# Where three weight tiles of a first layer are converted: beside that layer's own tiles, or between the joins of the second layer's first half

## The chip, the cores and the metric

One core of a Trainium2 chip runs the whole program. The metric is device time in microseconds (us). Engines are named as the profile names them: PE is the tensor engine (PEld its weight loads), DVE the vector engine, ACT the scalar engine, POOL the GpSimd engine, SP the engine from whose queue nearly all DMA transfers are issued.

## The reference

Four batch elements of 768 tokens go through two blocks.

```python
# block 1: 8 heads of 64 channels; each query sees its neighbours closer than 16 tokens,
# and 24 summaries (maximum of keys, mean of values over blocks of 32 tokens)
a = softmax([scale * q @ k.T within the window, scale * q @ k_sum.T + log(32)])
x = a @ [v, v_sum]                        # laid out as (4, 768, 512)
# block 2
u = x + real(fft(fft(x, axis=1), axis=2))
un = (u - mean(u)) / sqrt(var(u) + 1e-6)
out = u + maximum(un @ w_ch1, 0) @ w_ch2  # w_ch1 512 x 2048, w_ch2 2048 x 512
```

The two weight matrices arrive as 64-bit floats. The kernel turns them into 32-bit floats itself, once, while it works on the first batch element.

## The kernel before, in words

**The work of a batch element.** Attention by pairs of heads (`scores`, `sum_scores`, `values`), the two Fourier transforms and the normalisation (`gen_fourier`), the first layer (`gen_hidden`) and the second layer (`gen_out`). Each layer is done in two halves: `gen_hidden(b, 0)`, `gen_out(b, 0)`, `gen_hidden(b, 1)`, `gen_out(b, 1)`. Attention of the next batch element runs between them; in the stretch that matters here that is batch element 1, its last pair of heads (`p_1_3`), beside the layers of batch element 0.

**The layers.** Both layers use Strassen's scheme with seven products in place of eight (in the form with shared sums), so each weight tile is stored as seven blocks: four of the matrix, of which one is overwritten, and sums of them. The first layer's hidden units are cut into eight tiles j = 0 to 7, each with one weight tile `w1_0_j`. `gen_hidden(0, 0)` does tiles 0 to 3, `gen_hidden(0, 1)` tiles 4 to 7: seven products each, into PSUM banks `hx`, `hy`, `hz` (L1450), with copies and Relu on ACT (L1461, L1466, L1468, L1458, L1477) and additions on DVE (L582, the helper `tt`). The second layer has eight weight tiles `w2_0_j` likewise; `gen_out(0, 0)` contracts over tiles 0 to 3 and `gen_out(0, 1)` over 4 to 7.

**The second layer's first half, `gen_out(0, 0)`.** It has three row steps. The first is plain, since the sums of `w2` are not there yet: two PSUM banks (`o_0_0_0`, `o_0_0_3`, L1721), each added into `x` by one DVE instruction. Then row steps i = 1 and 2 do seven products each (L1746) into banks `ox`, `oy`, `oz`, and after each product a *join* on DVE adds the bank into `x`. The bank X is used by four products of a row step in turn, so each of them can begin only when the join of the one before has read it. There are four such banks in all (`bank`, `bufs=4`), and the bank of `o_0_0_3` is the one that the first product of row step 2 gets. Between the plain step and the rows DVE also makes the last sum T3 of each `w2` tile, and SP then stores the sums (`dw2_j`, 768 KB each).

**A conversion.** `convert(m)` turns one tile of 64-bit words into 32-bit floats. Its instructions on 128 x 1024 elements are: mask of the exponent bits (DVE, L1174), their shift (ACT, L1175), mask of the mantissa (DVE, L1187), its scaling (ACT, L1188), sign onto exponent (DVE, L1190), low word added (DVE, L1192), and the product (DVE, L582). `make` then adds three sums on DVE (L582, `_left_sums`). The raw words lie in a ring of two (`words`): the two loads of tile m + 2 can be issued once L1192 of tile m has read its words. SP issues transfers in a fixed order, and a transfer that waits holds all behind it.

**What sets the order.** `plan` (L1151) lists the sixteen conversions in order, each with a stage. `gen_weights` does not hand out a conversion before its stage is in `issued`. If the stage also has an entry in `marks`, the conversion's instructions are queued behind that instruction on the same engine (`tc.issue_after`). A scheduler then sets the order on each engine by what is handed out and by priority; each engine works strictly through its own list. Before the change, tiles 4, 5 and 6 of the first layer have the stages `("h", 0, 1)`, `("h", 0, 2)`, `("h", 0, 3)`, which are set at the end of tiles 1, 2, 3 of `gen_hidden(0, 0)`, and have no entry in `marks`.

## Time and profile before

| | |
|---|---|
| time, median of 3 runs | 794.03 us (792.45 to 794.19) |
| time of the profiled execution | 794.12 us |
| its span | 792.3 us (1.8 us lie outside the span) |
| PE, DVE, ACT busy | 767.6, 541.1, 248.9 us |
| mean clock granted to PE | 0.986 |

A row of the timeline gives the start, the duration, engine, line, operation, output and inputs, how many instructions were merged, and in brackets how long the engine sat idle before and whose end released it. A row of the windows gives, for a stretch of time, its length, the busy time of PE, PEld, DVE, ACT and POOL with the count of instructions, the clock granted to PE (1.00 is full), the share of the DMA engines and GB/s. One matrix product of the program is two records in the trace. The length of a record includes a tail that overlaps the next one; the time that a product takes of PE is the distance between starts.

### The profile page before, as it was taken

To read this page: it belongs to the slowest core of one execution; us is meant where nothing else is said; L and a number is where in the kernel's file an instruction comes from. 1 tells how busy PE (TensorE), PEld (TensorE's weight loads), DVE (VectorE), ACT (ScalarE), POOL (GpSimd) and SP (SyncE) were. 2 spreads that over 40 slices of the span, in tenths; PEclk is the share of its full clock that TensorE was granted. 3 is DMA by queue.
4 is the path that set the end of the run, shared out by engine and by line. 5 is a ranking of instruction groups with operands and counts; after the bars stand their busy time and mean duration, and the time that the engine had idled before them with its cause. 6 is when DMAs were issued, how large, how long until landed. Compare 5 with 4: busy or idle time off the path is not lost.

```text
span 792.3 us, 14996 instructions
## 1 busy us (share of the span) xinstructions
PE 767.6 (97%) x6068; PEld 591.0 (75%) x6068; DVE 541.1 (68%) x1145; ACT 248.9 (31%) x579; POOL 74.3 (9%) x102
## 2 busy tenths in 40 slices
PE   8999999869999999999999999999999999999997
PEld 5777555557569876688669876688659889889986
DVE  4789999976988825464576726463476987756762
ACT  3755657232535212200126112210116214203300
POOL 1000000000000002300030002300030004201500
PEclk8999999969999999999999999999999999999999
DMA  9897879695884359966244149820614034204001
GB/s 201 227 247 176 182 239 259 204 271 195 223 220 143 92 172 244 182 97 161 93 183 153 41 147 200 220 95 27 251 48 156 27 145 188 93 1 186 0 29 57
DMA packets 135901, 120.36 MB, mean 152 GB/s; under 512 B 94512, under 2 KB 117904, under 8 KB 135824
## 3 DMA queue, kind: packets, MB, share of 16 engines
q1 hardware_dynamic: 134672, 117.05, 53.6%
q0 software_dynamic: 576, 2.10, 0.8%
q8 instruction: 50, 0.82, 0.4%
q10 hardware_dynamic: 576, 0.17, 0.1%
q14 instruction: 27, 0.22, 0.1%
HBM read 97.28 MB, written 22.02 MB: 151 GB/s over the span
## 4 chain that ended last, share of the span: by engine, by line
PE 80%; DVE 12%; ACT 3%; DMA 2%; issue 1%; SPq 0%; DVEq 0%
PE ox L1746 19%; PE hx L1450 13%; PE oz L1746 10%; PE hz L1450 6%; PE oy L1746 5%; PE t L1619 4%; PE hy L1450 3%; PE y L1323 3%; DVE w L582 2%; PE f L1619 2%; PE mx L1282 2%; DMA words<-in_moe_w_ch_dram 2%; PE sc L810 2%; DVE w L1192 2%; PE sc L750 1%
## 5 line engine op out<-in xcount | busy, mean ns | idle before, releaser
L1450 PE MATMUL hx<-u,w 128*128 128x384 f32 x384 | 139.8, 492 | 1.2 <-ACT h L1461 0.8
L1450 PEld LDWEIGHTS hx<-u,w 128*128 128x128 f32 x384 | 71.1, 190 | 52.9 <-ACT p L817 3.7
L1746 PE MATMUL ox<-w,h 128*128 128x256 f32 x368 | 87.5, 382 | 4.1 <-DVE x L582 4.1
L1746 PE MATMUL ox<-w,s 128*128 128x256 f32 x368 | 89.3, 385 | 0.0
L1746 PE MATMUL oz<-w,s 128*128 128x256 f32 x368 | 89.0, 380 | 0.0
L1746 PEld LDWEIGHTS ox<-w,h 128*128 128x128 f32 x368 | 69.5, 191 | 16.1 <-DVE x L582 4.3
L1746 PEld LDWEIGHTS ox<-w,s 128*128 128x128 f32 x368 | 70.2, 193 | 10.6 <-DVE x L582 0.8
L582 DVE TENSOR_TENSOR x<-ox,x 128x256 f32<-128x256 f32 x92 | 38.9, 423 | 56.3 <-PE ox L1746 56.0
L1746 PEld LDWEIGHTS oz<-w,s 128*128 128x128 f32 x368 | 69.6, 190 | 9.5 <-DVE x L582 0.4
L1450 PE MATMUL hz<-u,w 128*128 128x384 f32 x192 | 70.3, 488 | 0.1
L1450 PEld LDWEIGHTS hz<-u,w 128*128 128x128 f32 x192 | 36.4, 190 | 25.6 <-DVE u L582 0.7
L1461 ACT COPY h<-hx 128x384 f32<-128x384 f32 x24 | 11.4, 476 | 114.0 <-PE hx L1450 114.0
L1746 PE MATMUL oy<-w,h 128*128 128x256 f32 x184 | 44.3, 381 | 0.7 <-ACT h L1668 0.7
L1622 ACT COPY f<-t 128x192 f32<-128x192 f32 x52 | 15.8, 303 | 78.3 <-PE t L1619 78.1
L582 DVE TENSOR_TENSOR x<-oz,x 128x256 f32<-128x256 f32 x46 | 19.5, 423 | 29.4 <-PE oz L1746 29.1
L1746 PEld LDWEIGHTS oy<-w,h 128*128 128x128 f32 x184 | 34.7, 190 | 6.2 <-ACT h L1668 1.5
L1598 POOL TENSOR_SCALAR h<-h 128x768 f32<-128x768 f32 x12 | 25.4, 2127 | 137.5 <-DVE h L1578 137.5
L585 POOL TENSOR_TENSOR vb<-vb 96x512 f32<-96x512 f32 (+2 forms) x20 | 20.4, 1022 | 174.2 <-DMA vb<-in_v_dram 173.2
L1450 PE MATMUL hy<-u,w 128*128 128x384 f32 x96 | 35.2, 488 | 1.5 <-DVE h L582 1.5
L582 DVE TENSOR_TENSOR s<-h 128x512 f32<-128x512 f32 x46 | 31.4, 682 | 0.9 <-ACT h L1458 0.6
L1477 ACT ACTIVATE h<-hx 128x384 f32<-128x384 f32 x24 | 11.7, 489 | 61.9 <-PE hx L1450 61.9
L582 DVE TENSOR_TENSOR h<-hy,h 128x384 f32<-128x384 f32 x24 | 13.3, 556 | 25.7 <-PE hy L1450 25.6
(236 smaller groups left out, 1310.5 us busy)
## 6 DMA issues: line engine op xcount, KB each, us to landing
w<-dw SPq DMA_DIRECT2D x46, 896.0 KB, 6.0
words<-in_moe_w_ch_dram SPq DMA_DIRECT2D x32, 512.0 KB, 6.0
dw<-w SPq DMA_DIRECT2D x12, 896.0 KB, 7.8
vw<-in_v_dram SPq DMA_DIRECT2D x47, 192.0 KB, 5.8
out_dram<-x SPq DMA_DIRECT2D x23, 256.0 KB, 2.0
vb<-in_v_dram SPq DMA_DIRECT2D x24, 192.0 KB, 8.1
kn<-in_k_dram SPq DMA_DIRECT2D x9, 384.0 KB, 6.4
qn<-in_q_dram SPq DMA_DIRECT2D x9, 384.0 KB, 7.2
```

Source lines behind the costliest of these rows:

```text
L582: return nc.vector.tensor_tensor(out=out, in0=in0, in1=in1, op=op).ins
L585: return nc.gpsimd.tensor_tensor(out=out, in0=in0, in1=in1, op=op).ins
L810: ins = nc.tensor.matmul(ps[h][r:r + 64, i, :], kt[rows, o:o + 64], qt[rows, o:o + BLOCK], start=True, stop=True)
L1192: nc.vector.scalar_tensor_tensor(out=dst, in0=low, scalar=2.0 ** -52, in1=dst, op0=ALU.mult, op1=ALU.add)
L1282: nc.tensor.matmul(out, y[:, g], table, start=False, stop=True, skip_group_check=True)
L1323: nc.tensor.matmul(y, fgs[b][par][:, st, P * g:P * (g + 1)], fs[par][:, g % 2, st, :], start=(st == 0), stop=(st == n - 1))
L1450: ins = nc.tensor.matmul(ps, w[:, a, kk, :], u[:, r, kk, :], start=start and kk == 0, stop=stop and kk == 1, skip_group_check=True)
L1477: nc.scalar.activation(out=c21, in_=X, func=AF.Relu)
L1598: nc.gpsimd.tensor_scalar(out=t, in0=t, scalar1=0.0, scalar2=None, op0=ALU.max)
L1619: marks["two"] = nc.tensor.matmul(o, left(j, a, m), rhs(r, m), start=m in (1, 5), stop=m in (2, 3, 4, 5, 7), skip_group_check=True).ins
L1622: nc.scalar.copy(out={1: f[:, 0], 6: f[:, 1], 7: g}[m], in_=t)
L1746: nc.tensor.matmul(ps, left[a][:, n, :], wt[2, b, j][:, r, :], start=start and n == 0, stop=stop and n == NC - 1, skip_group_check=True)
```

## The change

The stages of the three conversions become `("row", 0)`, `("row", 1)` and `("row", 2)`. A new function `pace` sets these stages inside `gen_out(0, 0)`: row 0 at the first join of the plain step, rows 1 and 2 after the second join of row steps 1 and 2. It also enters that join into `marks`, so that the conversion's DVE instructions are queued behind it. Nothing is computed that was not computed before, and no instruction is added on PE, DVE, ACT or POOL.

```diff
-            (2, 2, ("mx", 0)), (2, 3, ("mx", 0)), (1, 4, ("h", 0, 1)), (1, 5, ("h", 0, 2)), (1, 6, ("h", 0, 3)),
+            (2, 2, ("mx", 0)), (2, 3, ("mx", 0)), (1, 4, ("row", 0)), (1, 5, ("row", 1)), (1, 6, ("row", 2)),
...
+        def pace(i, ins):
+            if ("row", i) not in issued:
+                marks["row", i] = ins
+                issued.add(("row", i))
...
-                tt(x[:, t, :], ps, x[:, t, :], ADD)
+                pace(0, tt(x[:, t, :], ps, x[:, t, :], ADD))
...
             join(x11, Y, x11, ADD)
+            if plain:
+                pace(i, marks["dense"])
             one_sum(b, c, i)
```

Line numbers of the changed kernel are 6 higher than before from L1711 on (L1746 is L1752), and 8 higher from L1758 on. The number behind a tile's name only tells buffers apart. The orders below list an engine's instructions one behind the other.

On DVE, at the second plain join: before, the joins of the plain step and of row step 1 stand behind the conversions of tiles 4, 5 and 6 (`w1_0_6` is the last of these).

```order
L1192 SCALAR_TENSOR_TENSOR w1_0_6_1632<-words_103,w1_0_6_1632 128x1024
L1174 TENSOR_SCALAR words_103<-words_103 128x1024
L582 TENSOR_TENSOR w1_0_6_1632<-w1_0_6_1632,words_103 128x1024
L582 TENSOR_TENSOR x_1_919<-av_1_2_0_1646,rec_79 128x2x3x64
L856 RECIPROCAL rec_79<-av_1_2_1_1647 128x6
L582 TENSOR_TENSOR w1_0_6_1632<-w1_0_6_1632 128x256
L582 TENSOR_TENSOR x_1_919<-av_1_2_1_1647,rec_79 128x2x3x64
L582 TENSOR_TENSOR w1_0_6_1632<-w1_0_6_1632 128x2x256
L582 TENSOR_TENSOR x_0_145<-o_0_0_3_1629,x_0_145 128x512
L582 TENSOR_TENSOR w1_0_6_1632<-w1_0_6_1632 128x256
L582 TENSOR_TENSOR w2_0_3_1504<-w2_0_3_1504 128x256
L582 TENSOR_TENSOR x_0_145<-ox_0_0_1_1728,x_0_145 128x256
```

In the changed kernel the same joins stand in the same company behind the conversion of tile 4 alone:

```order
L1192 SCALAR_TENSOR_TENSOR w1_0_4_1604<-words_103,w1_0_4_1604 128x1024
L1174 TENSOR_SCALAR words_103<-words_103 128x1024
L582 TENSOR_TENSOR w1_0_4_1604<-w1_0_4_1604,words_103 128x1024
L582 TENSOR_TENSOR x_1_919<-av_1_2_0_1618,rec_79 128x2x3x64
L856 RECIPROCAL rec_79<-av_1_2_1_1619 128x6
L582 TENSOR_TENSOR w1_0_4_1604<-w1_0_4_1604 128x256
L582 TENSOR_TENSOR x_1_919<-av_1_2_1_1619,rec_79 128x2x3x64
L582 TENSOR_TENSOR w1_0_4_1604<-w1_0_4_1604 128x2x256
L582 TENSOR_TENSOR x_0_145<-o_0_0_3_1601,x_0_145 128x512
L582 TENSOR_TENSOR w1_0_4_1604<-w1_0_4_1604 128x256
L582 TENSOR_TENSOR w2_0_3_1504<-w2_0_3_1504 128x256
L582 TENSOR_TENSOR x_0_145<-ox_0_0_1_1700,x_0_145 128x256
```

The conversions of tiles 5 and 6 follow after these rows, with the remaining joins between their instructions. On DVE from the third join of row step 1 on:

```order
L582 TENSOR_TENSOR x_0_145<-oy_0_0_1_1701,x_0_145 128x256
L1187 TENSOR_SCALAR w1_0_5_1714<-words_103 128x1024
L1190 SCALAR_TENSOR_TENSOR words_103<-words_103 128x1024
L582 TENSOR_TENSOR x_0_145<-ox_0_0_1_1700,x_0_145 128x256
L1192 SCALAR_TENSOR_TENSOR w1_0_5_1714<-words_103,w1_0_5_1714 128x1024
L582 TENSOR_TENSOR s5_0_0_2_1754<-s4_0_0_2_1753,h_0_0_1255 128x512
L582 TENSOR_TENSOR w1_0_5_1714<-w1_0_5_1714,words_103 128x1024
L582 TENSOR_TENSOR x_0_145<-ox_0_0_1_1700,x_0_145 128x256
L582 TENSOR_TENSOR x_0_145<-oz_0_0_1_1702,x_0_145 128x256
L582 TENSOR_TENSOR w1_0_5_1714<-w1_0_5_1714 128x256
L1174 TENSOR_SCALAR words_103<-words_103 128x1024
```

Here one to two conversion instructions stand ahead of each join. On PE before, behind the third product of row step 1 stand the scores of `p_1_3`, and then, up to the second X product:

```order
L828 MATMUL ss_1_3_1843<-qt_1_3_1554,km1_83 32x384 x4
L710 MATMUL qk_2_0_0_1912<-ident_72,kn_2_0_1233 128x128 x3
L710 MATMUL qk_2_0_1_1918<-ident_72,kn_2_0_1233 128x128 x3
L710 MATMUL qk_2_0_0_1924<-ident_72,qn_2_0_1235 128x128 x3
L710 MATMUL qk_2_0_1_1930<-ident_72,qn_2_0_1235 128x128 x3
L834 MATMUL vs_1_3_1937<-vbs_1_1_1237,sel_75 128x64
L1746 MATMUL ox_0_0_2_1775<-w2_0_0_1250,h_0_0_1255 128x256
L1746 MATMUL ox_0_0_1_1728<-w2_0_0_1250,s5_0_0_1_1721 128x256
```

In the changed kernel the second X product follows at once; the scores come after row step 1, and the transposes `qk_2_0` and `vs_1_3` inside tile 4 of `gen_hidden(0, 1)`:

```order
L1752 MATMUL oz_0_0_1_1702<-w2_0_3_1504,s4_0_0_1_1692 128x256
L1752 MATMUL ox_0_0_2_1761<-w2_0_0_1250,h_0_0_1255 128x256
L1752 MATMUL ox_0_0_2_1761<-w2_0_1_1382,h_0_0_1255 128x256
L1752 MATMUL ox_0_0_2_1761<-w2_0_2_1415,h_0_0_1255 128x256
L1752 MATMUL ox_0_0_1_1700<-w2_0_0_1250,s5_0_0_1_1693 128x256
```

On SP before, the two loads of the raw words of tile 6 stand between the stores of `w2_0_0` and `w2_0_1`:

```order
L562 DMA dw2_0_95<-w2_0_0_1250 128x1536
L562 DMA words_103<-in_moe_w_ch1_dram 128x4x256 x2
L562 DMA dw2_1_96<-w2_0_1_1382 128x1536
L562 DMA words_103<-in_moe_w_ch2_dram 128x1024 x2
L562 DMA dw2_2_97<-w2_0_2_1415 128x1536
```

In the changed kernel the second of these loads stands behind the store of `w2_0_3`, which waits for that tile's T3 on DVE:

```order
L562 DMA dw2_0_95<-w2_0_0_1250 128x1536
L562 DMA dw2_1_96<-w2_0_1_1382 128x1536
L562 DMA dw2_2_97<-w2_0_2_1415 128x1536
L562 DMA dw2_2_97<-w2_0_2_1415 128x256
L562 DMA words_103<-in_moe_w_ch1_dram 128x4x256
L562 DMA dw2_3_98<-w2_0_3_1504 128x1536
L562 DMA words_103<-in_moe_w_ch1_dram 128x4x256
```

The three stores before it have moved ahead of both loads. POOL's order is unchanged. Behind tile 5 of `gen_hidden(0, 1)` PE's order is the one of before.

## The prediction

> **What bounds the kernel now.** I read the page first, then the busy time by stage, then the timelines of PE, DVE and ACT around the one stage in which PE rests. The page says that PE is the bound nearly everywhere:

> ```profile
> span 792.3 us, 14996 instructions
> PE 767.6 (97%) x6068; PEld 591.0 (75%) x6068; DVE 541.1 (68%) x1145; ACT 248.9 (31%) x579; POOL 74.3 (9%) x102
> ```

> So the kernel gets faster only where PE is idle or slow: 792.3 - 767.6 = 24.7 us of idle time. A third of it lies in one stretch of the windows (columns: length, busy PE, PEld, DVE, ACT, POOL, clock, DMA share, GB/s):

> ```profile
> 148.00:170.00 22.00, 13.35 (x147) 9.36 (x146) 20.14 (x33) 12.15 (x20) 0.00 (x0) 0.75 0.75 228
> 170.00:190.00 20.00, 20.00 (x88) 17.30 (x88) 11.68 (x22) 1.84 (x2) 0.00 (x0) 0.94 0.73 214
> 190.00:230.00 40.00, 38.79 (x222) 22.84 (x221) 33.77 (x53) 20.06 (x36) 0.00 (x0) 1.00 0.80 225
> 230.00:270.00 40.00, 39.79 (x226) 35.85 (x225) 34.97 (x93) 18.04 (x53) 0.74 (x1) 1.00 0.54 144
> ```

> From 148 to 170 PE is idle for 22.00 - 13.35 = 8.65 us while DVE is full (20.14 of 22), and in the next stretch it is the other way round: PE is full, DVE is free for 8.3 of 20 us. PE's timeline shows where the idle time lies, and what follows:

> ```profile
> 128.32 0.82 PE L710 MATMUL qk<-ident,kn 128*128 128x128 f32 x6
> 128.98 0.82 PE L710 MATMUL qk<-ident,qn 128*128 128x128 f32 x6
> ...
> 151.75 1.89 PE L1746 MATMUL oz<-w,s 128*128 128x256 f32 x8
> ...
> 160.68 0.90 PE L710 MATMUL qk<-ident,kn 128*128 128x128 f32 x3 [3.60 <-ACT p L829]
> ...
> 168.55 1.22 PE L1746 MATMUL ox<-w,h 128*128 128x256 f32 x2 [4.13 <-DVE x L582]
> ...
> 189.67 1.45 PE L1450 MATMUL hx<-u,w 128*128 128x384 f32 x4
> 190.96 1.45 PE L1450 MATMUL hy<-u,w 128*128 128x384 f32 x4
> ...
> 213.43 1.56 PE L1450 MATMUL hx<-u,w 128*128 128x384 f32 x4 [0.75 <-ACT h L1461]
> ...
> 216.74 1.56 PE L1450 MATMUL hx<-u,w 128*128 128x384 f32 x4 [0.46 <-ACT h L1466]
> ...
> 229.74 1.89 PE L1746 MATMUL ox<-w,h 128*128 128x256 f32 x8
> 231.47 1.89 PE L1746 MATMUL oy<-w,h 128*128 128x256 f32 x8
> ```

> Two waits make up 3.60 + 4.13 = 7.73 of the 8.65 us. The second is released by a join on DVE. DVE's timeline says why that join was late:

> ```profile
> 151.00 1.22 DVE L582 TENSOR_TENSOR w<-w,words 128x1024 f32<-128x1024 f32 x1
> 152.14 0.69 DVE L1187 TENSOR_SCALAR w<-words 128x1024 int32<-128x1024 int32 x1
> 152.74 0.42 DVE L582 TENSOR_TENSOR w<-w 128x256 f32<-128x256 f32 x1
> 153.08 1.24 DVE L1190 SCALAR_TENSOR_TENSOR words<-words 128x1024 int32<-128x1024 int32 x1
> ...
> 165.87 0.55 DVE L582 TENSOR_TENSOR x<-av,rec 128x384 f32<-128x384 f32 x1
> ...
> 167.81 0.69 DVE L582 TENSOR_TENSOR x<-o,x 128x512 f32<-128x512 f32 x1
> ...
> 169.07 0.42 DVE L582 TENSOR_TENSOR x<-ox,x 128x256 f32<-128x256 f32 x1
> ...
> 169.74 0.42 DVE L582 TENSOR_TENSOR x<-oy,x 128x256 f32<-128x256 f32 x1
> ...
> 224.64 0.41 DVE L582 TENSOR_TENSOR w<-w 128x256 f32<-128x256 f32 x1
> ```

> The join of `o_0_0_3` at 167.81 frees the bank that PE needs at 168.55. Its product was done long before; ahead of it in DVE's list stood, from 152.14 to 165.87, the conversions of tiles 5 and 6. The first wait has the same source at one remove. On ACT:

> ```profile
> 158.16 1.15 ACT L1175 ACTIVATE words<-words,rebias 128x1024 int32<-128x1024 int32 x1 [2.08 <-DVE words L1174]
> 159.21 1.04 ACT L1188 ACTIVATE w<-w 128x1024 f32<-128x1024 int32 x1
> 160.16 0.47 ACT L829 ACTIVATE p<-ss 128x384 f32<-128x384 f32 x1
> 160.53 2.11 ACT L713 COPY kt<-qk 64x384 f32<-64x384 f32 x4
> ```

> The exponential of the summary scores (L829), for which PE's transposes wait, stands behind tile 6's two ACT instructions, and these wait for DVE. A third cost is the clock that PE was granted:

> ```profile
> 157.00:159.00 2.00, 0.08 (x1) 0.00 (x0) 2.00 (x5) 0.84 (x1) 0.00 (x0) 0.97 1.00 224
> 159.00:171.00 12.00, 5.85 (x17) 3.70 (x18) 10.14 (x20) 7.20 (x14) 0.00 (x0) 0.50 0.86 286
> 171.00:173.00 2.00, 2.00 (x7) 1.68 (x6) 1.83 (x3) 0.00 (x0) 0.00 (x0) 0.62 1.01 243
> ```

> After about 2 us of rest the clock fell to 0.50 and came back at about 172.5 (0.62 over the last 2 us means half clock for 1.5 of them). PE was busy at half clock for 5.85 + 1.5 = 7.35 us, so 3.7 us of that were lost.

> **The change, part by part.** *What goes.* If the joins come when their products are done, both waits, the small ones beside them and the slow clock go: 8.65 + 3.7 = 12.35 us. The work on PE itself is unchanged; the twelve transposes and the vs product are moved from the stall to tile 4 of the first layer's second half, where at full clock they take 2 x 0.66 us by the two qk rows at 128. They count as work in both places.

> *What is late next: the join of `o_0_0_3`.* DVE's list is the old one up to the product of tile 4 at 151.00. Then, where L1187 of tile 5 stood at 152.14, stands now what stood at 165.87. With the old distances (1.94 to the plain join, 3.20 to the first X join, 3.87 to the Y join) these begin at 154.08, 155.34 and 156.01; the plain join ends at 154.77. A product of four steps takes PE 1.73 us (229.74 to 231.47), so PE is through with the Z product at 151.75 + 1.73 = 153.48 and wants the bank. New wait: **1.3 us**. Nothing covers it, as these DVE rows are all measured.

> *The other joins.* The conversions of tiles 5 and 6 now lie between joins, so that each join may wait for one or two conversion instructions, 0.6 us (L1187, by the distance 152.14 to 152.74) or 1.1 us each (L1190, 151.00 to 152.14 for the product). PE has other products to do meanwhile: after the X product that is released at 155.8 it is busy to 158.7, and the next X join, behind L1187 and L1190 of tile 5, ends at 158.5; the one after that ends at 161.7, and PE comes at 162.2. Cover of 0.2 and 0.5 us, so I cost these at nothing; without the cover each would be one conversion instruction, about 1.1 us.

> *The queue of SP.* The second half of tile 6's words is now issued behind the store of `w2_0_3`. That store waits for T3 on DVE, which stands ahead of the X join and ends by 155.4; the load goes out at about 156. What such a load takes is told by the DMA list at three times (issues between 201 and 203, 150 and 152, 155 and 157 us; last figure: us to landing):

> ```profile
> words<-in_moe_w_ch_dram SPq DMA_DIRECT2D x1, 512.0 KB, 3.5
> ...
> words<-in_moe_w_ch_dram SPq DMA_DIRECT2D x2, 512.0 KB, 5.3
> ...
> words<-in_moe_w_ch_dram SPq DMA_DIRECT2D x2, 512.0 KB, 7.1
> ```

> So it lands between 159.9 and 163.5. DVE comes to L1174 of tile 6 at 162.3, in the midst of joins: a wait of 0 to 1.2 us, and what is queued behind it are the joins of row step 2, with next to no cover at the second X join. It cannot help, so nothing below zero; I take **0.6 us**, between the second and the third row, since a 768 KB store goes just ahead. [...]

> *The second half of the first layer.* There DVE and ACT gain no work but the moved transposes' eight copies (4.2 us on ACT by the row at 160.53), and yet the stage starts with less done ahead. Worked forward with the durations above, ACT's list between the exponents of tile 7 (from 182.0) and the first copy of hx of tile 5 is those copies, two small ones, three Relu, and two L1175 and one L1188 (1.05 and 0.95 each): it is through at 191.4, where PE wants it at 190.2. That is 1.2 us. In the same way 0.5 us come out before the fourth product of tile 5, and 2.1 us in tile 6, where the copy of hx stands behind L1188 of `w2_0_6`, whose words are loaded late. Before there were 0.75 + 0.46 = 1.21 us in this stage. Net new wait: 3.8 - 1.2 = **2.6 us**; the least is 0, the most is the first rival.

> *Sum*, against the profiled execution's 794.12 us (within 0.1 us of the median 794.03): 12.35 - 1.3 - 0.6 - 2.6 = 7.85 us less, **786.3 us**. Behind 230 us both kernels run one PE list that waits for almost nothing, so I expect the rest to move as a whole.

> **Rivals.** *1. Given back by the conversions that follow.* `gen_out(0, 1)` needs tiles 4 to 7 of the second layer in its first product. Before, the last sum of the last tile ended at 224.64 + 0.41 = 225.05 and PE began at 229.74: 4.7 us of slack. If DVE, ACT and the loads do not finish this chain any earlier, PE waits there, and the gain is just the slack: 794.1 - 4.7 = 789.4 us. For it speaks that DVE is busy 33.77 of 40 us in that stage, and that each load waits for an older conversion; against it the 8.3 us in which DVE is free from 170 to 190, which tiles 5 and 6 now use.

> *2. Slower: the clock stays low.* PE now rests often and briefly. If such rests held the clock at 0.50 through the two row steps, their 22 us of PE work (154.8 to 177.0) would take 22 us longer: 786.3 + 22 = 808 us. It decides from 7.85 us of such loss, 16 us at half clock. [...] Against it speak the two stretches with rests of 0.75 and 0.46 us, at full clock:

> ```profile
> 213.00:214.00 1.00, 0.57 (x2) 0.44 (x3) 1.00 (x2) 0.38 (x2) 0.00 (x0) 1.00 1.22 238
> 216.00:218.00 2.00, 1.54 (x5) 0.87 (x5) 2.00 (x4) 2.00 (x5) 0.00 (x0) 1.00 1.42 126
> ```

> *3. No change: the transfers become the bound.* From 190 to 230 the DMA engines are busy 0.80 x 40 = 32 us; with 7.85 us less there is room for 32.15. If more has to land before PE may go on (tables of the next Fourier transform, raw words), all of the gain can be eaten: 794 us. Against it: the share is 0.54 after 230, so there is room behind.

> **How the numbers follow.** The forecast has 0.75, the first rival 0.16, the slow clock 0.04, the transfers 0.03; 0.02 stay for what I do not see, split between the sides. The forecast's own best end is the sum with the two uncertain terms at 0: 794.12 - 12.35 + 1.3 = 783.1 us. Its worst end meets the first rival, at 789.4 us. The range is these two ends, and leaves out the last two rivals. A measurement of this kernel can tell about 0.2%, 1.6 us, from no change. Faster: 0.75 + 0.16 + 0.01 = 0.92; within 0.2%: 0.03; slower: 0.04 + 0.01 = 0.05.

> **What would show it.** Right: the plain join of `o_0_0_3` begins near 154.1 and PE waits for it 1 to 1.5 us; no window of the two row steps shows a clock below 1.00; the first layer's second half begins near 177 to 178; `gen_out(0, 1)` starts 7 to 9 us earlier than 229.74. Wrong: an L1174 that waits over 1.5 us for words between joins; PE waiting for a `w2` tile at the start of `gen_out(0, 1)` (first rival); a clock of 0.50 with no rest over 2 us ahead (second); PE rests behind that point which were not there before (third).

## The result, and the profile after

| | before | after |
|---|---|---|
| median beside each other | 793.24 us (791.03 to 794.19) | 781.95 us |
| ratio | | 0.985, 95% interval 0.981 to 0.990 |
| profiled execution, span | 794.12, 792.3 us | 780.33, 778.5 us |
| mean clock granted to PE | 0.986 | 0.996 |

One execution of the changed kernel took 4474 us; it is left out of the ratio but not of the median, which is 780.33 us without it. The change makes the kernel about 1.5% faster. The forecast was 786.3 us with a range from 783.1 to 789.4, so the direction was right and the size too small: the median lies 1.2 us below the range. The ratio's interval, applied to the 794.12 us from which the sum started, is 779 to 786 us.

The page of the changed kernel:

```profile
span 778.5 us, 14991 instructions
PE 762.0 (98%) x6068; PEld 586.6 (75%) x6068; DVE 539.7 (69%) x1145; ACT 248.7 (32%) x579; POOL 74.7 (10%) x102
```

Idle time of PE fell from 24.7 to 16.5 us, and its busy time by 5.6 us with the same 6068 instructions, at a mean clock of 0.996 instead of 0.986. The windows (same columns as before) show where:

```profile
148.00:170.00 22.00, 20.72 (x188) 16.95 (x187) 21.54 (x40) 5.87 (x8) 0.00 (x0) 1.00 0.88 228
170.00:190.00 20.00, 19.07 (x73) 12.09 (x71) 16.43 (x25) 13.38 (x24) 0.00 (x0) 1.00 0.70 233
190.00:230.00 40.00, 39.04 (x251) 27.45 (x251) 36.94 (x61) 16.89 (x40) 0.74 (x1) 1.00 0.72 217
```

From 148 to 170 PE is idle for 1.3 us instead of 8.65, at a clock of 1.00 instead of 0.75, and DVE now works through the stretch from 170 to 190 too. PE's timeline (in brackets the wait and whose end released it):

```profile
147.91 1.89 PE L1752 MATMUL oz<-w,s 128*128 128x256 f32 x8
150.97 1.56 PE L1752 MATMUL ox<-w,h 128*128 128x256 f32 x6 [1.17 <-DVE x L582]
...
178.12 0.82 PE L710 MATMUL qk<-ident,kn 128*128 128x128 f32 x6
...
188.07 1.56 PE L1450 MATMUL hx<-u,w 128*128 128x384 f32 x4 [0.93 <-ACT h L1461]
...
190.20 0.33 PE L846 MATMUL av<-vw,p 64*32 64x65 f32 x12
190.54 1.56 PE L1450 MATMUL hx<-u,w 128*128 128x384 f32 x4
...
200.11 1.56 PE L1450 MATMUL hx<-u,w 128*128 128x384 f32 x4 [0.78 <-ACT h L1461]
...
215.69 1.89 PE L1752 MATMUL ox<-w,h 128*128 128x256 f32 x8
```

DVE's timeline:

```profile
150.24 0.68 DVE L582 TENSOR_TENSOR x<-o,x 128x512 f32<-128x512 f32 x1
...
152.50 0.68 DVE L1187 TENSOR_SCALAR w<-words 128x1024 int32<-128x1024 int32 x1
...
158.51 0.68 DVE L1174 TENSOR_SCALAR words<-words 128x1024 int32<-128x1024 int32 x1
...
195.82 0.68 DVE L1174 TENSOR_SCALAR words<-words 128x1024 int32<-128x1024 int32 x1
...
210.12 1.60 DVE L582 TENSOR_TENSOR w<-w 128x512 f32<-128x512 f32 x3
```

The join of `o_0_0_3` begins 2.33 us behind the start of row step 1's Z product (150.24 - 147.91), to the hundredth the distance that the sum had (154.08 - 151.75). No L1174 of the stretch has a bracket: none waits for words.

**What the change did, and what the execution did.** The two profiled executions differ by 13.8 us, which is more than the change is worth. Up to the Z product at 147.91 PE, DVE, ACT and POOL run the same instructions in the same order in both kernels, and yet the changed kernel comes there 3.84 us earlier (before: 151.75). 3.81 us of this are there at 101.73 us already (97.92 in the changed kernel), long before SP's orders part. So the change is read from that point to the start of `gen_out(0, 1)`. The kernel before, two stretches: from there to `gen_out(0, 1)`, and from there to the end:

```profile
151.75:229.74 77.99, 68.13 (x435) 46.16 (x434) 61.63 (x100) 32.30 (x54) 0.00 (x0) 0.91 0.81 234
229.74:792.30 562.56, 556.19 (x4075) 448.43 (x4073) 349.11 (x785) 129.53 (x352) 69.97 (x87) 1.00 0.43 124
```

The changed kernel, the same two:

```profile
147.91:215.69 67.78, 64.78 (x435) 43.81 (x434) 60.75 (x100) 32.13 (x54) 0.00 (x0) 1.00 0.82 244
215.69:778.50 562.81, 556.23 (x4075) 447.59 (x4073) 348.67 (x785) 129.63 (x352) 70.41 (x87) 1.00 0.43 124
```

The first stretch is 10.2 us shorter: 6.9 us less idle (9.86 to 3.00) and 3.35 us less busy for the same 435 records. The second is the same within 0.3 us: the rest moved as a whole.

### The profile page after: what moved, and what is told of

Same layout as the page of the kernel before. It is cut to its first block, busy times and chain, and to the rows that moved or that the text cites. A ratio compares the mean times of both kernels' runs of the same rounds, so it can differ in the third digit from the quotient of the medians.

```text
span 778.5 us, 14991 instructions
## 1 busy us (share of the span) xinstructions
PE 762.0 (98%) x6068; PEld 586.6 (75%) x6068; DVE 539.7 (69%) x1145; ACT 248.7 (32%) x579; POOL 74.7 (10%) x102
## 4 chain that ended last, share of the span: by engine, by line
PE 83%; DVE 10%; ACT 4%; DMA 1%; issue 1%; SPq 0%; DVEq 0%; ACTq 0%
PE ox L1752 18%; PE hx L1450 14%; PE oz L1752 9%; PE hz L1450 7%; PE oy L1752 5%; PE t L1619 4%; PE hy L1450 3%; PE y L1323 3%; DVE w L582 2%; PE sc L810 2%; PE f L1619 2%; PE mx L1282 2%; PE av L846 2%; DVE w L1192 1%; PE av L851 1%
## 5 line engine op out<-in xcount | busy, mean ns | idle before, releaser
L1450 PE MATMUL hx<-u,w 128*128 128x384 f32 x384 | 140.0, 492 | 1.7 <-ACT h L1461 1.7
L1450 PEld LDWEIGHTS hx<-u,w 128*128 128x128 f32 x384 | 70.8, 190 | 53.0 <-ACT h L1461 3.8
L1752 PE MATMUL oz<-w,s 128*128 128x256 f32 x368 | 88.9, 380 | 0.0
L1752 PE MATMUL ox<-w,h 128*128 128x256 f32 x368 | 87.1, 380 | 1.2 <-DVE x L582 1.2
L1752 PE MATMUL ox<-w,s 128*128 128x256 f32 x368 | 87.9, 380 | 0.1
L1752 PEld LDWEIGHTS ox<-w,h 128*128 128x128 f32 x368 | 69.1, 190 | 13.7 <-issue 1.7
L1752 PEld LDWEIGHTS ox<-w,s 128*128 128x128 f32 x368 | 69.0, 190 | 10.9 <-DVE x L582 0.8
L1752 PEld LDWEIGHTS oz<-w,s 128*128 128x128 f32 x368 | 69.4, 190 | 9.7 <-DVE x L582 0.4
L582 DVE TENSOR_TENSOR x<-ox,x 128x256 f32<-128x256 f32 x92 | 38.8, 422 | 52.1 <-PE ox L1752 51.7
L1450 PE MATMUL hz<-u,w 128*128 128x384 f32 x192 | 70.4, 487 | 0.0
L1450 PEld LDWEIGHTS hz<-u,w 128*128 128x128 f32 x192 | 36.3, 190 | 25.0
L1461 ACT COPY h<-hx 128x384 f32<-128x384 f32 x24 | 11.5, 478 | 114.0 <-PE hx L1450 114.0
L1752 PE MATMUL oy<-w,h 128*128 128x256 f32 x184 | 44.5, 380 | 0.7 <-ACT h L1668 0.7
L1752 PEld LDWEIGHTS oy<-w,h 128*128 128x128 f32 x184 | 34.7, 190 | 6.3 <-ACT h L1668 1.5
L582 DVE TENSOR_TENSOR x<-oz,x 128x256 f32<-128x256 f32 x46 | 19.4, 422 | 27.4 <-PE oz L1752 27.1
L1450 PE MATMUL hy<-u,w 128*128 128x384 f32 x96 | 35.2, 488 | 0.0
L582 DVE TENSOR_TENSOR s<-h 128x512 f32<-128x512 f32 x46 | 31.3, 681 | 0.9 <-ACT h L1458 0.6
L582 DVE TENSOR_TENSOR h<-hy,h 128x384 f32<-128x384 f32 x24 | 13.3, 555 | 25.9 <-PE hy L1450 25.8
## 6 DMA issues: line engine op xcount, KB each, us to landing
words<-in_moe_w_ch_dram SPq DMA_DIRECT2D x32, 512.0 KB, 5.5
```

Of the source, the lines that this page charges most:

```text
L582: return nc.vector.tensor_tensor(out=out, in0=in0, in1=in1, op=op).ins
L1450: ins = nc.tensor.matmul(ps, w[:, a, kk, :], u[:, r, kk, :], start=start and kk == 0, stop=stop and kk == 1, skip_group_check=True)
L1752: nc.tensor.matmul(ps, left[a][:, n, :], wt[2, b, j][:, r, :], start=start and n == 0, stop=stop and n == NC - 1, skip_group_check=True)
```

## The experiments

The theory, A: PE stood because DVE's list, and through it ACT's, had the conversions of tiles 5 and 6 ahead of all joins of row step 1 and of the exponential of the summary scores; the rest of PE also cost it the clock. One row of the kernel before, which the prediction does not show, belongs to that list:

```profile
164.13 0.69 DVE L1174 TENSOR_SCALAR words<-words 128x1024 int32<-128x1024 int32 x1 [1.86 <-DMA words<-in_moe_w_ch_dram]
```

Here DVE itself stood, ahead of all these joins, until the raw words of the second layer's tile 4 had landed (2.42 us in again_before). So of the 13.7 us between 152.14 and 165.87, which the prediction puts down to the conversions of tiles 5 and 6, 1.9 are a wait for a transfer. Neither the changed kernel nor only6 nor join_first has this wait. In join_first, where tiles 5 and 6 stand as before, the X join is late even without it, so the conversions are the larger part.

Rivals are stated with each run. All were timed in five rounds beside the kernel before. The last column is the stretch from the start of row step 1's Y product (1.72 us ahead of the Z product, and in all kernels the same point of the program) to the start of `gen_out(0, 1)`, in the profiled execution.

| run | median, us | before, us | ratio, 95% interval | stretch, us |
|---|---|---|---|---|
| kernel before (again_before) | 791.8 | 792.16 | 1.001, 0.999 to 1.002 | 79.7; again 79.3 |
| changed kernel (again_after) | 781.8 | 792.16 | 0.987, 0.984 to 0.990 | 69.5; again 69.5 |
| five_six | 781.96 | 792.16 | 0.988, 0.986 to 0.991 | 69.8 |
| row0_second | 781.16 | 792.16 | 0.986, 0.983 to 0.989 | 68.2 |
| no_marks | 781.81 | 791.5 | 0.987, 0.985 to 0.989 | 69.1 |
| only6 | 782.38 | 791.5 | 0.989, 0.987 to 0.991 | 71.9 |
| dve_copies | 781.75 | 791.5 | 0.987, 0.985 to 0.989 | 68.5 |
| fill_stall | 794.72 | 791.5 | 1.004, 1.003 to 1.006 | 83.1 |
| join_first | 788.19 | 791.4 | 0.995, 0.993 to 0.996 | 76.0 |
| fill_shorter | 796.63 | 791.4 | 1.006, 1.003 to 1.008 | 85.1 |
| store_twice | 780.37 | 791.4 | 0.986, 0.983 to 0.988 | 68.8 |
| best | 778.66 | 791.4 | 0.983, 0.981 to 0.986 | 67.6 |
| fill_vs | 789.03 | 792.99 | 0.996, 0.994 to 0.998 | 78.5 |
| store_ahead | 781.58 | 792.99 | 0.984, 0.982 to 0.987 | 68.8 |

**again_before and again_after: the two kernels, unaltered, once more.**

> The kernel before once more, unaltered, as a control. Theory A: ratio 1.000 within 0.003, and its profile may reach the Z product of row step 1 anywhere from 147 to 152 us. Theory B: its profile reaches it at 151 to 152 us again.

> The changed kernel once more, unaltered, to get its interval and a second profile. Theory A: the change is worth what the two traces show between the Z product of row step 1 and the start of gen_out(0, 1), 78.0 us before and 67.8 after, so 10.2 us; the further 3.8 us by which the first profile after was ahead before the change begins belong to that execution. Then the median lies 9.5 to 11 us under the kernel before, ratio 0.986 to 0.988, and the second profile again has about 67.8 us in that stretch, whatever its start took. Theory B: the change also moves the part ahead of it (placement of code or data): then the median lies 13 to 14.5 us under, ratio 0.982 to 0.984, and the second profile reaches the Z product near 147.9 again.

In the second pair the stretch from the Z product is, for the kernel before:

```profile
148.71:226.31 77.60, 67.86 (x436) 45.96 (x435) 61.48 (x100) 32.27 (x54) 0.00 (x0) 0.91 0.79 236
```

and for the changed kernel:

```profile
150.06:217.81 67.75, 64.76 (x436) 43.81 (x434) 60.75 (x100) 32.11 (x54) 0.00 (x0) 1.00 0.81 243
```

So 9.85 us, as in the first pair (10.2). Here the changed kernel is the one that comes later to the Z product (150.06 against 148.71): the 3.84 us of the first pair belong to the execution. Of the change's 10.0 us on average, 6.8 are idle time and 3.2 are clock.

**five_six, no_marks, row0_second: which part of the change is needed.** five_six gives tile 4 its old stage; no_marks sets the stages but makes no entry in `marks`; row0_second releases tile 4 at the second plain join instead of the first.

```diff
 five_six
-(1, 4, ("row", 0)), (1, 5, ("row", 1)), (1, 6, ("row", 2))
+(1, 4, ("h", 0, 1)), (1, 5, ("row", 1)), (1, 6, ("row", 2))
 no_marks, in pace
-                marks["row", i] = ins
 row0_second
-                pace(0, tt(x[:, t, :], ps, x[:, t, :], ADD))
+                ins = tt(x[:, t, :], ps, x[:, t, :], ADD)
+                if t:
+                    pace(0, ins)
```

> Tile 4 keeps its old stage, tiles 5 and 6 have the new ones. Stall theory: what matters is what stands on DVE ahead of the second plain join, and there tile 4 stands either way; so the same time as the changed kernel within 1 us, 10 us under the kernel before. Rival (each tile moved is worth a third): 6 to 7 us under the kernel before.

> The three stages are released by the joins as in the change, but the joins are not entered into marks, so the conversions are not queued behind them. Theory A (only the place in DVE's list ahead of the join of o_0_0_3 matters, and that is the same): as the changed kernel, 10 to 10.5 us less than before. Rival B (the tie to the joins is what keeps them on time): at least 1 us slower than the changed kernel, and waits of PE for joins of row steps 1 and 2 which the changed kernel does not have.

> Stage row 0 is set at the second plain join and not at the first, so that tile 4 too stands behind the join of o_0_0_3. Stall theory: the wait of 1.17 us at that join goes; if nothing else is late, 1.2 us less than the changed kernel, 11 us under the kernel before. Rival (given back): the conversions now end some 5 us of DVE work later against the joins, and PE waits between joins or at the start of the second half: 0 to 3 us more than the changed kernel.

Tile 4's stage and the tie by `marks` make no difference that can be measured (69.8 and 69.1 against 69.5 us). What counts is when tiles 5 and 6 are handed out, and of the two mostly tile 6, as only6 below shows. row0_second gains 1.3 us more in its stretch. Its DVE timeline has the join of `o_0_0_3` ahead of tile 4's conversion:

```profile
147.27 0.69 DVE L582 TENSOR_TENSOR x<-o,x 128x512 f32<-128x512 f32 x1
147.87 0.69 DVE L1187 TENSOR_SCALAR w<-words 128x1024 int32<-128x1024 int32 x1
```

and PE no longer waits for that bank, which is the 1.17 us of the changed kernel. Its median does not stand out from the changed kernel's.

**only6 and join_first: how much of the list is the cause.** only6 moves tile 6 alone; join_first takes the kernel before and raises one join, that of `o_0_0_3`, ahead of the conversions.

```diff
 only6, against the changed kernel
-(1, 4, ("row", 0)), (1, 5, ("row", 1)), (1, 6, ("row", 2))
+(1, 4, ("h", 0, 1)), (1, 5, ("h", 0, 2)), (1, 6, ("row", 2))
 join_first, against the kernel before
-                tt(x[:, t, :], ps, x[:, t, :], ADD)
+                with tc.high_priority(600):
+                    tt(x[:, t, :], ps, x[:, t, :], ADD)
```

> Only the sixth-indexed tile is moved (tile 6 to row 2), tiles 4 and 5 keep their old stages, so that on DVE the join of o_0_0_3 stands behind tile 5's conversion as well. Theory A (the stall is the length of DVE's and ACT's lists ahead of that join and of the exponential of the summary scores): by the distances of before the join begins 8.6 us behind the start of row step 1's Z product (before 16.1, changed kernel 2.3), and PE is held by the twelve transposes instead, whose exponential comes one ACT instruction earlier; PE starts row step 2's first product about 11.7 us behind that Z product (before 16.8). With less slow clock behind it that is 5.5 to 7 us less than before. Rival B (what counts is how much conversion work lies in the stage, a third of it moved): a third of the gain, 3 to 4 us less.

> The kernel before with one thing changed: the join of o_0_0_3 has a higher priority, and stands on DVE behind L1192 of tile 4, ahead of the conversions of tiles 5 and 6; the joins of row step 1 stay behind them. Rival B (that one join is the blocker, since it frees the bank of row step 2): nearly the whole gain, 8 to 10 us less than before. Theory A (all joins of row step 1 are held by the same conversions, so the wait goes on to the next): PE does row step 2's first product (1.7 us) before the summary scores, then waits for the X join of row step 1, which begins about where it did before: 1 to 2.5 us less than before.

PE's timeline of only6:

```profile
147.01 1.89 PE L1752 MATMUL oz<-w,s 128*128 128x256 f32 x8
...
154.22 0.90 PE L710 MATMUL qk<-ident,kn 128*128 128x128 f32 x3 [1.89 <-DVE x L582]
...
156.90 2.02 PE L1752 MATMUL ox<-w,h 128*128 128x256 f32 x4
```

The product of row step 2 starts 9.9 us behind the Z product, not 11.7 as I had worked out, since the transposes began earlier and went faster than I had them; by the trace 7.6 us are gained, somewhat over A's range, and far over the third that the rival had. Tile 6 alone is thus worth about three quarters of the change's 10.0 us. PE's timeline of join_first:

```profile
151.77 1.89 PE L1747 MATMUL ox<-w,h 128*128 128x256 f32 x8
157.48 0.85 PE L828 MATMUL ss<-qt,km 64*32 64x384 f32 x8 [2.29 <-ACT p L817]
...
165.90 3.78 PE L1747 MATMUL ox<-w,s 128*128 128x256 f32 x8 [3.01 <-DVE x L582]
```

The bank of `o_0_0_3` is free at once (no bracket at 151.77), and PE then stands before the next product, for the next join. So that one join was not the blocker: the conversions ahead of all of row step 1's joins were. The gain of 3.5 us by the trace is over the 1 to 2.5 that A gave: A had the X join where it was before, and it began 15.3 us behind the Z product instead of 17.3 and 17.9, about as much sooner as DVE stood for words in the two traces of before (1.86 and 2.42).

**dve_copies: the wait in the first layer's second half.** The changed kernel with the eight copies of the moved transposes on DVE:

```diff
-                    nc.scalar.copy(out=dst[...], in_=ps[...])
+                    (nc.vector.tensor_copy if (b, g) == (2, 0) else nc.scalar.copy)(out=dst[...], in_=ps[...])
```

> The changed kernel, with the eight copies of the moved transposes (kt and qt of batch element 2, pair 0) on DVE instead of ACT. Theory A (the wait of 0.93 us for the copy of hx in the first layer's tile 5 stands behind these copies in ACT's list): that wait goes, and the kernel is 0.5 to 1 us faster than the changed one, 10.7 to 11.5 us less than before. Rival B (DVE, which has the conversions there, becomes late instead): a wait for DVE of the same size or more in its place, no faster or slower than the changed kernel.

ACT's timeline of the changed kernel shows what it is about:

```profile
179.75 2.08 ACT L713 COPY kt<-qk 64x384 f32<-64x384 f32 x4
181.85 2.08 ACT L713 COPY qt<-qk 64x384 f32<-64x384 f32 x4
...
187.53 0.48 ACT L1461 COPY h<-hx 128x384 f32<-128x384 f32 x1
```

With the copies away, the waits of 0.93 and 0.78 us for L1461 are gone, one of 0.40 us is left and one of 0.21 us for DVE's copies is new, and the stretch is 0.95 us shorter, as A had it. The median is not: the profiled execution is 1.7 us longer behind `gen_out(0, 1)` than that of the changed kernel (564.5 against 562.8 us). That the cause of the wait is ACT's list is shown; that removing it alone pays is not.

**fill_stall, fill_shorter, fill_vs: the price of the slow clock.** Matmuls of 128 x 128 that nobody reads are added to the kernel before, into unused columns of a bank: 14 behind the summary scores and 18 behind the vs product; 12 and 18; none and 10.

```diff
+    def fill(ps, n):
+        with tc.high_priority():
+            for _ in range(n): nc.tensor.matmul(ps[:, S2:512], ident, ident, start=True, stop=True)
...
+        fill(ps, 10 * ((b, g) == (1, 3)))     # in scale_sums, behind the vs product
```

> The kernel before, with 14 matmuls of 128x128 that nobody reads put into PE's list behind the summary scores and 18 behind the vs product, about 3.0 and 3.9 us at full clock, so that PE works through most of its two waits. Nothing else is moved, and the joins come no earlier. Theory A (the slow clock comes from PE's rest and is a cost of its own): the clock stays at 1.00 from 157 to 173 us, and the products behind the second wait, which took 4 us at half clock, take 2: 1.5 to 2.5 us less than before although PE does more. Rival B (the slow clock only stretches work that would wait anyway, or does not come from the rest): no difference, within 0.5 us, or slower by what the added matmuls hang over.

> fill_stall with 12 instead of 14 matmuls behind the summary scores, with which the transposes get the same banks as before, so that they do not wait for DVE's work on av. Work that nobody reads is added to PE, nothing else; the joins come no earlier. Theory A (the slow clock comes from PE's rest and is a cost of its own): the clock stays at 1.00 from 157 to 173 us, and 1 to 1.8 us less than before. Rival B (it is not, or the fall of the clock does not come from the rest): no less than before, and a clock of 0.50 in the products behind the second wait.

> The kernel before with ten matmuls of 128x128 that nobody reads behind the vs product, and none behind the summary scores; every bank and every wait ahead of them is as in the kernel before, so that they fall into PE's second wait. At half clock they take 4.3 to 4.8 us, about the wait's length. In the traces so far the clock came back at the end of the first stretch of 3.4 us in which PE worked without a rest, and the instants at which it changed lie a multiple of 3.41 us apart. Theory A (the slow clock is a cost of its own, and PE's rest keeps it low): PE is busy from the vs product on, the clock is back at 1.00 between 167.5 and 171 us instead of 169.5 to 172.5, and the products behind the wait lose 0.5 us instead of 2 to 2.6: 1 to 2 us less than before. Rival B (the slow clock costs nothing of its own, or work that nobody reads does not bring it back): no less than before, or up to 0.5 us more.

The first two do not answer the question. PE got a new wait for DVE in front of the last transposes (4.95 us, fill_stall) or of the vs product (4.14 us, fill_shorter). I put it down to a changed choice of banks, which is not shown, as the trace does not name the banks:

```profile
162.16 0.90 PE L711 MATMUL qk<-ident,qn 128*128 128x128 f32 x3 [4.95 <-DVE x L583]
163.17 5.79 PE L581 MATMUL vs<-ident 128*128 128x128 f32 x36
```

(fill_stall; its lines are numbered one higher.) The matmuls behind the vs product then stood in front of the products, and both kernels were slower, by 3.6 and 5.5 us in the stretch. fill_vs has no such new wait. Its PE timeline, and then its windows of 3.41 us:

```profile
159.89 4.40 PE L581 MATMUL vs<-ident 128*128 128x128 f32 x20
165.45 1.56 PE L1747 MATMUL ox<-w,h 128*128 128x256 f32 x6 [1.16 <-DVE x L583]
```

```profile
157.14:160.56 3.42, 2.96 (x11) 2.16 (x12) 0.87 (x1) 2.63 (x6) 0.00 (x0) 0.50 0.98 392
160.56:163.97 3.41, 3.41 (x18) 3.41 (x17) 2.94 (x6) 1.65 (x2) 0.00 (x0) 0.50 0.98 309
163.97:167.38 3.41, 2.25 (x12) 1.86 (x11) 3.41 (x9) 0.52 (x2) 0.00 (x0) 1.00 0.29 88
```

The clock is back 1.5 us ahead of the product that waits, where before it came back 4.0 us behind it. The ratio is 0.994 to 0.998, and the stretch is 0.8 to 1.2 us shorter, although the join came 0.6 to 1.1 us later there. From the product's start to `gen_out(0, 1)` it is 58.8 us (before 61.2 and 60.3), and PE is busy there for 58.05 us instead of 59.98 and 59.71 with the same products. PE does more work and the kernel is faster: the slow clock has a price of its own, as A said. That the timing shows more (1.7 to 4.8 us) than this stretch is not explained.

**store_twice and store_ahead: SP's queue.** In the changed kernel the second half of tile 6's words went out at 151.98 behind a store. Its row in the trace of that tile says:

```profile
DMA to landing us min/median/max: 5.3/5.3/5.3
```

So it landed at 157.3, and L1174 read it at 158.51: a cover of 1.2 us. Both kernels add a second store of 768 KB, store_ahead to memory of its own.

```diff
 store_ahead, against the changed kernel
+    spare = dpool.tile([P, 7, HD], FP, name="spare")
...
+                if j == js[-1]: fetch(out=spare[:, 1:7], in_=w[:, 1:7])
                 fetch(out=dw2[j][:, 1:7], in_=w[:, 1:7])
```

> The changed kernel with the store of three quarters of w2_0_3 (768 KB) issued twice, so that more stands ahead of tile 6's raw words at the DMA engines. In the changed kernel these words landed 5.3 us after their issue, 1.2 us before L1174 of tile 6 read them. Theory A (the term of SP's queue is real and was covered by these 1.2 us): the second store costs 2 to 3.5 us of transfer, L1174 waits 0.8 to 2.3 us, the joins behind it wait with it, and the kernel is 0.5 to 2.5 us slower than the changed one. Rival B (the load shares the DMA engines with the store and lands hardly later): no wait at L1174, within 0.3 us of the changed kernel.

> The changed kernel with a second store of 768 KB of w2_0_3, to memory that nobody reads, in SP's list ahead of the first one and so ahead of the second half of tile 6's raw words. L1174 of tile 6 stands some 2 us later in DVE's list than in the changed kernel, by the list's durations at about 13 us behind the start of row step 1's Z product (10.6 there). Theory A (bytes ahead in the queue delay the load): it lands 7.3 to 8.5 us after its issue instead of 5.3, and L1174 waits 0 to 1 us; 0 to 1.2 us slower than the changed kernel. Rival B (the load shares the DMA engines and lands hardly later): about 5.3 us after its issue, no wait, within 0.7 us of the changed kernel.

In store_twice the second store, to the same memory as the first, stands behind the load; the load landed after 5.3 us again, and the run says nothing on bytes ahead. In store_ahead two stores stand ahead, and the same line reads:

```profile
DMA to landing us min/median/max: 7.1/7.1/7.1
```

1.8 us later. L1174 stood 2.5 us later in DVE's list than in the changed kernel, and did not wait. At its old place, 10.6 us behind the Z product, it would have waited 1.0 us (landing 161.9; 150.24 + 10.6 = 160.8). So in these two traces the load landed later with more bytes ahead (7.1 against 5.3 us), and in the changed kernel the cover of 1.2 us was enough. No loss shows: the stretch is 68.8 us, against 69.5 in the changed kernel.

**best: row0_second and dve_copies together.**

> row0_second (tile 4 released by the second plain join) and dve_copies together. Theory A (each takes away a wait of PE of its own: 1.17 us at the bank of o_0_0_3, and 0.93 us behind the eight copies on ACT): between row step 1's second product and the start of gen_out(0, 1) about 2.2 us less than in the changed kernel (1.3 by the trace of row0_second, 0.9 by that of dve_copies), 12 to 12.6 us less than before. Rival B (the chain of conversions ahead of gen_out(0, 1) is now the bound, as my first rival said): PE waits for a w2 tile there, and no more than 11 us less than before.

```profile
169.02 1.99 PE L1754 MATMUL oz<-w,s 128*128 128x256 f32 x8 [0.40 <-DVE x L582]
...
190.41 1.56 PE L1450 MATMUL hx<-u,w 128*128 128x384 f32 x4 [0.82 <-ACT h L1466]
```

These are its two largest waits before `gen_out(0, 1)`. The stretch is 1.9 us shorter than the changed kernel's, a little under the 2.2 expected, and the median is 12.7 us below the kernel before, just above A's 12 to 12.6; PE does not wait for a `w2` tile. It beats the kernel before by 1.4 to 2.0%. That it beats the changed one rests on the 1.9 us of the trace alone, as the intervals of the two ratios overlap.

## Why the prediction was too cautious, step by step

- **What goes, 12.35 us.** Idle time: all 8.65 us went (the wait for raw words, shown above, with them). Clock: 3.7 us forecast, 3.2 measured by the busy time of the same records. Together 11.9.
- **Join of `o_0_0_3`, 1.3 us.** Measured 1.17. Right, and row0_second shows its cause.
- **Other joins, nothing.** Right: all other rests in the stretch come to 0.12 us (3.00 - 1.17 - 0.93 - 0.78).
- **SP's queue, 0.6 us.** Measured 0. The load went out and L1174 came about when forecast (4.1 and 10.6 us behind the Z product), and the load took 5.3 us, the middle one of the three rows. I had taken the middle of the waits at the ends instead (0 and 1.2), and at the middle row the wait was already 0.
- **The first layer's second half, 2.6 us net.** This is the step that failed. Measured 1.71 - 1.21 = 0.5. Of its three places the first was nearly right (1.2 forecast, 0.93). The second, 0.5 us before the fourth product of tile 5, does not show: twelve matmuls of `values`, which I had left out, stand there in PE's list (190.20) and take 0.34 of it. The third, 2.1 us in tile 6, was 0.78: I had the words of `w2_0_6` late, and they were not (L1174 at 195.82 does not wait).
- **Sum.** 11.9 - 1.17 - 0 - 0.5 - 0.1 = 10.1 us, against 10.0 measured in the stretch and 7.85 forecast. The mechanism was the right one, and the miss of 2.2 us is these terms.
- **The base.** The sum was taken from one execution at 794.12 us. In the runs on the chip the kernel before had medians of 791.4 to 793.2. That is where the other 0.9 to 2.7 us come from; 794.12 - 10.0 = 784.1 would have lain inside the range. The range held the uncertain terms and no spread of the base, which the three times given (792.45 to 794.19) already showed.
- **Rivals.** First: the last sum of the last tile ended at 211.7 and PE began at 215.69, so 4.0 us of slack were left of 4.7; nothing was given back. Second: the clock is 1.00 in the whole stretch. Third: the part behind 215.69 is as long as before.

## What to carry to other kernels

When a helper's work stands ahead of the consumer that the critical engine waits for, ask for every item between the two, not for the one whose end releases the wait: raising one join only moved the wait to the next (join_first), and handing the helper's work out later moved them all. Work a chain of new waits forward only with everything that stands in the lists, fillers too, and where three rows give a price, go with the middle row through to the wait rather than average the waits. Measure a change between two points of the program that both kernels pass, and give the base a spread of its own.

## What was not expected of the hardware

```profile
152.06:155.47 3.41, 3.12 (x104) 2.55 (x102) 3.41 (x6) 1.53 (x3) 0.00 (x0) 1.00 0.94 246
155.47:158.89 3.42, 1.32 (x11) 0.46 (x11) 3.42 (x6) 1.34 (x3) 0.00 (x0) 1.00 1.07 323
158.89:162.30 3.41, 1.60 (x6) 1.00 (x6) 3.37 (x5) 3.32 (x7) 0.00 (x0) 0.50 0.92 255
162.30:165.71 3.41, 1.80 (x6) 1.01 (x5) 1.58 (x2) 2.68 (x5) 0.00 (x0) 0.50 1.02 425
165.71:169.13 3.42, 0.58 (x1) 0.50 (x2) 3.42 (x10) 1.31 (x4) 0.00 (x0) 0.50 0.78 203
169.13:172.54 3.41, 3.41 (x9) 2.46 (x8) 3.41 (x8) 0.00 (x0) 0.00 (x0) 0.50 0.74 233
172.54:175.95 3.41, 3.41 (x17) 3.00 (x17) 2.49 (x5) 0.00 (x0) 0.00 (x0) 1.00 1.19 225
```

It fell at 158.89, at the end of a window in which PE was busy for 1.32 of 3.41 us, and came back at 172.54, at the end of the first full one. In seven traces (before, again_before, only6, join_first and the three fills) the time at half clock in this stretch was 6.83, 10.24 or 13.65 us, that is 2, 3 or 4 times 3.41. In join_first a rest of 2.29 us (155.19 to 157.48) lay across two windows. The first kept 2.48 us of work, and the clock stayed; the second, with the other part of the rest and one of 0.38 us, kept 1.68, and the clock fell at its end:

```profile
152.71:156.12 3.41, 2.48 (x101) 1.99 (x99) 3.41 (x5) 0.75 (x2) 0.00 (x0) 1.00 1.01 365
156.12:159.54 3.42, 1.68 (x14) 0.77 (x14) 3.42 (x5) 3.41 (x7) 0.00 (x0) 1.00 1.01 402
```

So in this trace two waits close together cost the clock. The changed kernel's three lie in windows of their own, the emptiest with 2.25 us of work, and its clock stayed at 1.00.

Cut in this way, ten falls of the clock in nine traces (one in each of the other six named above, after and again_after, two in before; their last 5 us left out) have windows ahead of them with 0.55 us (fill_vs) to 1.70 us of work (fill_shorter). The clock stayed after windows with 1.95 us (fill_vs, 150.32 to 153.73) and, with a wait of 1.68 us in it, 1.7 us of work (fill_shorter, up to 203.40). A sharp limit is not shown: other falls, such as those behind a clock of 0.72 to 0.86 from 10 to 20 us in five traces, are not among the ten. After each of the ten the clock came back at the end of a window that was full; one with 3.06 us of work was not enough (again_after, 76.24 to 79.65 us). A full one was not always enough either: in the kernel before PE was busy for all 3.41 us from 8.70 to 12.11, and the clock came back at 15.53, at the end of the second full one. PE ran mostly small matmuls in the first (tiles of 64 x 96 and 64 x 32); why it was not enough is not shown.

The slow clock is part of why one execution differs from the next. In the first profile of the kernel before the clock was 0.50 from 8.70 to 15.53 us, and one and the same matmul of the attention then starts at 18.11 us, against 14.86 in the changed kernel. But the changed kernel's profile has a clock of 0.50 from 76.17 to 79.59 us, and gives part of this back. Together the two make, by my estimate, up to 1.7 us, half of 6.83 - 3.41, of the 3.84 us at the common point. The rest of it is not traced.
